# An attention and maxout kernel: its opening stage written as one list of pieces, with its PSUM places rearranged

## The chip, the cores and the metric

One NeuronCore of a Trainium2 chip runs one launch. The metric is device time in microseconds (us); less is better. Three runs of the kernel before took 813.16 to 813.38 us, with a median of 813.33.

## What is computed

```python
def mab(q, kv):                                  # scale = 1 / sqrt(128)
    s = scale * (q @ kv.transpose(0, 2, 1))
    s = s - s.max(-1, keepdims=True)
    a = np.exp(s); a /= a.sum(-1, keepdims=True) + 1e-09
    return a @ kv
h = mab(I, x)             # 32 inducing rows attend to 12544 tokens; 4 batches, 128 channels
y = mab(x, h)             # every token attends to the 32 rows of h
z = np.maximum(np.maximum(y @ w1, y @ w2), y @ w3)   # 128 -> 768
out = z @ w_out                                   # 768 -> 128
```

Everything is float32. The weights lie in memory as 64-bit floats.

## The kernel before, in words

A batch is 98 tiles of 128 tokens: group 0 has two tiles ("short": `xgs`, `xTs`), groups 1 to 6 have 16 (`xg`, `xT`). The program has two stages. The **opening stage** (`phase1_first` and the `ORDER` loop behind it) computes `h` of batch 0 from its seven groups, converts the weights from 64 to 32 bits, and makes the product `us` of `h` with the weights. The **main stage** (`main`, `advance`, `stage2`) takes 512 tokens at a time through the second attention and the maxout in 600 slots, and works out `h` of the next batch in between. Every engine runs its instructions in the order in which the code records them (`manual_schedule`), so an order is written out by hand, for the opening stage in `LOADS`, `WORK` and `ORDER`.

In the opening stage each group g goes through these steps; the letters are those of the changed list:

- l: a load of the SP queue. 0 to 6 are the token groups, 7 is w2, 8 is w_out, 9 is w1, 10 is w3. Full groups have four buffers; group 5 has one of its own, and group 6 takes that of group 1 once its sums are done.
- T: TensorE transposes 4 tiles (`transpose_x`, L343); C: ScalarE copies them out of PSUM (L345). Four of each for a full group.
- S: scores, inducing rows times tokens (`attend_products`, L353). M: their maximum on VectorE (L391). D: a column of it on ScalarE (L398). P: one small matmul that spreads it over the partitions (`attend_spread`, L405). L: the least of it on VectorE (L410).
- E: exponentials on ScalarE (L436). V: their transpose on VectorE (L465). U: the weighted sums of tokens on TensorE (`attend_sums`, L489). K: ScalarE keeps them (`attend_keep`, L502).
- w0 to w3 with a letter: conversion of a weight (0 w2, 1 w_out, 2 w1, 3 w3): t (L240), T (L244), p (L249) and r (L253) on VectorE, z (L259) on ScalarE, A (L261) an addition on GpSimd or VectorE, d (L265) on VectorE, S (L269) on GpSimd.

Then `cl`, `cw`, `cm`, c and `sg`, `ts`, `it`, `cs` combine the seven groups into `hT` (L616 to L663). Behind it come scores of batch 0 (`scores_products`, L734), four matmuls f0 to f3 to `us` (L677, `first_products`), their copies h and z (L682, L692) and differences v, scores e0, e1 of batch 1 (L353, groups 0 and 1), the copy `ek` of those (L374), the steps a and b of the second softmax of groups 0 and 1 (L747 to L783), and the first slots of the main stage (s, `advance`). The copies `pT` of finished weights (`probs`, L803) go over the SP queue.

PSUM has eight banks: `aux0`, `aux1`, `pu0`, `pu1`, `pv0`, `pv1`, `acc0`, `acc1`. Before, scores alternate between the two `aux` banks, the spread maximum has `acc0` and the sums have `acc1`.

```python
for gi in range(NG - 1):
    attend_products(0, gi + 1, bank_a[(gi + 1) % 2])
    attend_weights(0, gi)
    ...
    attend_spread(0, bank_o[0])
    attend_least(0, gi + 1)
```

Of the kernel before, what the change touches and what calls it, by code (L numbers as in the profile page):

```python
# [25 lines left out]
def kernel(ctx, tc, x, xt, ind_t, w1, w2, w3, w_out, out):  # L26
    nc = tc.nc
# [11 lines left out]
    LOADS = (0, 1, 2, 7, 3, 8, 4, 5, 9, 6, 10)  # L39

    WORK = (
        "",
        ("0t 0T 0p 0z", "0r 0A"),
        ("1t 1T 1p 1z", "1r 1A"),
        ("0d 1d", "2t"),
        ("2T 2p 2z", "2r 2A"),
        ("3t 3T 3z", "3p 2d 2S"),
        "3r",
        "3a 3d 3S",
    )  # L50
# [142 lines left out]
    raws = []  # L193
    def first_loads():
        for what in LOADS:
            if what < NG:
                xg_next[(0, what)] = load_group(0, what, pieces=4 if what == 1 else 1)
            else:
                raws.append(load_raw(srcs[what - NG]))
# [75 lines left out]
    def work(steps):  # L275
        for kind in steps.split():
            convert(int(kind[0]), kind[1])

    w2t = []

    def transpose_w2():
        for h in range(2):
            tpw = bank_v[h]
            for k in range(3):
                j = 3 * h + k
                nc.tensor.transpose(out=tpw[:, k * P : (k + 1) * P], in_=wf[:, 0, j * P : (j + 1) * P], identity=ident)
            w2h = hp.tile([P, 512], F32, name="w2h", tag="ru", bufs=3)
            nc.scalar.copy(out=w2h[:, : 3 * P], in_=tpw[:, : 3 * P])
            w2t.extend(w2h[:, k * P : (k + 1) * P] for k in range(3))
# [86 lines left out]
    def attend_max(b, gi):  # L376
# [15 lines left out]
        st["mq"] = mq  # L392

    def attend_column(b):

# [1 line left out]
        md = wk.tile([P, NQ], F32, name="md", tag="md")
        nc.scalar.mul(out=md, in_=quad, mul=st["mq"])  # L398
        st["md"] = md

    def attend_spread(b, bank=None):
# [143 lines left out]
    def phase1_first():  # L545

        start_batch(0)
        nc.sync.dma_start(out=iT, in_=ind_t)
        nc.scalar.mul(out=iT, in_=iT, mul=scale)
        first_loads()  # L550
        def half(gi, k):
            if gi < NG:
                if k == 0:
                    start_group(0, gi)
                for i in (k, k + 4):
                    transpose_x(0, gi, i)

        start_group(0, 0)
        keep_busy(6, bank_o[1])
        transpose_x(0, 0, 0)  # L560
        keep_busy(2, bank_o[1])
        attend_products(0, 0, bank_a[0])
        attend_max(0, 0)
        attend_column(0)
        half(1, 0)
        attend_spread(0, bank_o[0])
        attend_least(0, 0)
        half(1, 8)
        work(WORK[0])
        st = state[0]  # L570
        for gi in range(NG - 1):
            last = gi == NG - 2
            attend_products(0, gi + 1, bank_a[(gi + 1) % 2])
            attend_weights(0, gi)
            if gi == 2:
                keep_busy(4, bank_o[1], P)
            half(gi + 2, 0)
            attend_max(0, gi + 1)
            attend_column(0)
            half(gi + 2, 8)  # L580
            if gi > 0:
                attend_sums(0, gi - 1, bank_o[1])
                attend_keep(0, gi - 1)
            attend_transpose(0, gi)
            if not last:
                work(WORK[gi + 1][0])
            attend_spread(0, bank_o[0])
            attend_least(0, gi + 1)
            if gi == 3:
                transpose_w2()  # L590
            if last:
                prep_products()
            else:
                work(WORK[gi + 1][1])
        combine_least(st)
        work(WORK[NG - 1])
        combine_weights(st)
        attend_weights(0, NG - 1)
        keep_products()
        attend_sums(0, NG - 2, bank_o[1])  # L600
        attend_keep(0, NG - 2)
        combine_mask(st)
        combine_groups(st, range(NG - 1), bank_u[0])
        attend_transpose(0, NG - 1)
        sum_groups(st)
        attend_sums(0, NG - 1, bank_o[1])
        total_sums(st, bank_o[0])
        attend_keep(0, NG - 1)
        work(WORK[NG])
        invert_total(st)  # L610
        combine_groups(st, range(NG - 1, NG))
        combine_states(st, NQ)

# [429 lines left out]

    with tc.manual_schedule(engines=MANUAL):
        phase1_first()
        st = state[0]
        scores_products(0, 0, bank_a[0])
        scores_products(0, 1, bank_a[1])
        prep_out()
        first_products(st, 0, bank_o[0])  # L1050
        first_products(st, 1, bank_o[1])
        start_batch(1)
        load_channels(1, 0)
        load_channels(1, 1)
        load_channels(1, 2)
# [1 line left out]
        for step in ORDER.split():
            if step == "p":
                chunks[0].pT = probs(chunks[0], bank_u[0])
            elif step == "q":  # L1060
                chunks[1].pT = probs(chunks[1])
            elif step == "d":
                keep_busy(2, bank_u[(pipe["next"] + 1) % 2])
            elif step == "s":
                advance()
            elif step == "S":
                scores_products(0, 2, bank_a[0])
            elif step == "e":
                attend_products(1, 1, bank_v[1])
                attend_products(1, 0, bank_v[0])  # L1070
            elif step == "f":
                keep_scores(1)
            elif step == "g":
                attend_products(1, 2, bank_a[1])
            elif step == "m":
                more = len(st["up"])
                first_products(st, more, bank_o[more - 2])
            elif step == "c":
                first_low(st, which)
            elif step in steps:  # L1080
                next(steps[step])
            else:
                which = int(step)
                first_high(st, which)
# [59 lines left out]
```

## Time and profile before

| what | value |
|---|---|
| time of three runs | 813.16, 813.33, 813.38 us |
| span of the profiled execution, first to last instruction | 811.8 us |
| so around the span, against the median | 1.5 us |
| TensorE busy | 800.6 us, 99% of the span |
| ScalarE, GpSimd, VectorE busy | 91%, 80%, 77% |
| granted TensorE clock | 1.000 over the span |

The profile gives the span of its execution and no time of its own; the three runs stand beside it. A line of the timeline reads: start, duration, engine (PE TensorE, PEld its weight loads, ACT ScalarE, DVE VectorE, POOL GpSimd, SPq the SP queue), line, operation, output<-input, shape, count, and in brackets the idle time of that engine before it with what ended it. Busy time is a share over stages with different limits, so the opening stage (about 0 to 55 us) has to be read apart from the rest.

### The profile page before, as it was taken

The numbers are of one execution on the slowest core, as the hardware profiler recorded it, in microseconds if no ns is written. First come the engines' busy times: TensorE is split into PE (matmuls) and PEld (weight loads), VectorE is DVE, ScalarE is ACT, GpSimd is POOL, SyncE is SP. The second block draws the span as 40 slices with busy tenths as digits, with TensorE's granted clock in tenths as the row PEclk, the third lists the DMA queues.
The fourth block names the chain that finished last, engine by engine and source line by source line (L and its number), as shares of the span: only waits on it lengthen the run. The fifth ranks groups of instructions, "written<-read, shape, count | busy, mean of one in ns | idle before, by whom it ended". The sixth has DMA issues, their size and how long they took to land.

```text
span 811.8 us, 14334 instructions
## 1 busy us (share of the span) xinstructions
PE 800.6 (99%) x4561; PEld 629.4 (78%) x4561; DVE 628.0 (77%) x1067; ACT 734.8 (91%) x1532; POOL 648.2 (80%) x520
## 2 busy tenths in 40 slices
PE   8989999999999999999999999999999999999998
PEld 5758778777777787787877877878878788787887
DVE  4878878777877887877886878778778778778874
ACT  6779889899998998988998989889989999899996
POOL 1269879788788887886987978878879889788887
PEclk9999999999999999999999999999999999999999
DMA  8843234274542633533734426334223222222221
GB/s 327 318 141 111 75 122 145 85 244 157 178 134 69 192 116 103 192 117 108 233 113 123 118 99 197 112 105 134 69 77 102 66 72 78 66 87 73 62 79 52
DMA packets 52842, 102.51 MB, mean 126 GB/s; under 512 B 18208, under 2 KB 22176, under 8 KB 47520
## 3 DMA queue, kind: packets, MB, share of 16 engines
q1 hardware_dynamic: 52624, 101.47, 39.6%
q8 instruction: 36, 0.59, 0.3%
q14 instruction: 38, 0.31, 0.1%
q10 hardware_dynamic: 144, 0.13, 0.0%
HBM read 48.12 MB, written 25.69 MB: 91 GB/s over the span
## 4 chain that ended last, share of the span: by engine, by line
PE 96%; DMA 2%; SPq 1%; issue 0%; ACT 0%; DVE 0%; POOL 0%; POOLq 0%; ACTq 0%; DVEq 0%
PE acc L885 17%; PE pu L820 17%; PE pv L826 17%; PE acc L886 16%; PE acc L887 16%; PE aux L734 3%; PE acc L884 3%; PE acc L489 3%; PE aux L353 2%; DMA xg<-in_x_dram 2%; PE pu L343 0%; SPq L169 0%; PE pv L343 0%; POOL us L693 0%; PE aux L700 0%
## 5 line engine op out<-in xcount | busy, mean ns | idle before, releaser
L850 POOL TENSOR_TENSOR lows<-h,hi 128x512 fp32r<-128x512 f32 (+1 forms) x504 | 633.5, 1291 | 122.1 <-ACT hi L842 121.4
L853 DVE TENSOR_TENSOR h<-pv,ru 128x512 f32<-128x512 f32 (+1 forms) x600 | 403.4, 674 | 159.1 <-PE pv L826 99.8
L835 ACT ACTIVATE ru<-pu 128x512 f32<-128x512 f32 (+1 forms) x600 | 387.3, 645 | 51.3 <-PE pu L820 49.0
L842 ACT CAST hi<-h 128x512 fp32r<-128x512 f32 (+1 forms) x600 | 398.6, 664 | 0.3 <-DVE h L853 0.3
L820 PE MATMUL pu<-pT,us 128*128 128x512 f32 (+1 forms) x600 | 231.8, 387 | 1.8 <-ACT hi L842 0.9
L885 PE MATMUL acc<-hi,wo_hi 128*128 128x512 f32 (+1 forms) x594 | 231.8, 390 | 0.0
L826 PE MATMUL pv<-pT,us 128*128 128x512 f32 (+1 forms) x600 | 231.8, 386 | 0.1
L886 PE MATMUL acc<-hi,wo_lo 128*128 128x512 f32 (+1 forms) x594 | 228.9, 385 | 0.0
L887 PE MATMUL acc<-lows,wo_hi 128*128 128x512 f32 (+1 forms) x594 | 228.8, 385 | 0.0
L885 PEld LDWEIGHTS acc<-hi,wo_hi 128*128 128x128 f32 x594 | 111.5, 188 | 29.3 <-issue 7.5
L820 PEld LDWEIGHTS pu<-pT,us 128*128 128x128 f32 x600 | 112.5, 188 | 26.8 <-ACT ru L835 1.5
L826 PEld LDWEIGHTS pv<-pT,us 128*128 128x128 f32 x600 | 112.6, 188 | 23.7 <-DVE h L853 1.2
L887 PEld LDWEIGHTS acc<-lows,wo_hi 128*128 128x128 f32 x594 | 111.5, 188 | 22.7
L886 PEld LDWEIGHTS acc<-hi,wo_lo 128*128 128x128 f32 x594 | 111.6, 188 | 21.7
L856 DVE TENSOR_TENSOR lows<-h,hi 128x512 fp32r<-128x512 f32 x96 | 76.5, 797 | 0.8 <-ACT hi L842 0.8
L898 ACT COPY o<-acc 128x512 f32<-128x512 f32 (+1 forms) x96 | 61.6, 641 | 0.0
L884 PE MATMUL acc<-pT,us 128*128 128x512 f32 (+1 forms) x99 | 38.1, 385 | 0.0
L489 PEld LDWEIGHTS acc<-xg,aT 128*32 128x32 f32 x672 | 18.7, 110 | 9.4 <-issue 5.8
L353 PE MATMUL aux<-xT,iT 128*32 128x512 f32 x184 | 24.2, 597 | 1.7 <-ACT xT L345 1.7
L734 PE MATMUL aux<-xT,hT 128*32 128x512 f32 x192 | 25.1, 603 | 0.0
L261 POOL TENSOR_TENSOR rest<-rest,t 128x768 f32<-128x768 f32 x3 | 5.5, 1819 | 24.4 <-DVE rest L253 24.4
L489 PE MATMUL acc<-xg,aT 128*32 128x128 f32 x672 | 22.5, 273 | 0.0
(151 smaller groups left out, 446.2 us busy)
## 6 DMA issues: line engine op xcount, KB each, us to landing
out_dram<-o SPq DMA_DIRECT2D x95, 256.0 KB, 2.2
xg<-in_x_dram SPq DMA_DIRECT2D x23, 1024.0 KB, 5.9
xT<-in_xt_dram SPq DMA_DIRECT2D x18, 1024.0 KB, 5.3
pT<-ph SPq DMA_DIRECT2D x192, 64.0 KB, 2.0
pT<-pl SPq DMA_DIRECT2D x192, 64.0 KB, 2.0
raw<-in_w_dram SPq DMA_DIRECT2D x3, 768.0 KB, 8.5
us<-uh SPq DMA_DIRECT2D x24, 52.0 KB, 1.9
us<-ul SPq DMA_DIRECT2D x24, 52.0 KB, 2.6
```

The source lines that it names most:

```text
L489: nc.tensor.matmul(out=hps[q * M : (q + 1) * M, :], lhsT=aT[g][:, t * M : (t + 1) * M], rhs=xgs[g][:, t, :], start=(first[q] == k), stop=( ...
L820: nc.tensor.matmul(out=pu[:, :w], lhsT=state[c.b]["us"][:, 2 * j * P : (2 * j + 1) * P], rhs=c.pT[:, :w], start=True, stop=True)
L826: nc.tensor.matmul(out=pv[:, : d.w], lhsT=state[d.b]["us"][:, (2 * j + 1) * P : (2 * j + 2) * P], rhs=d.pT[:, : d.w], start=True, stop=True,)
L835: nc.scalar.activation(out=ru[:, :w], in_=pu[:, :w], func=AF.Relu)
L842: nc.scalar.copy(out=hi[:, : c.w], in_=h[:, : c.w])
L850: nc.gpsimd.tensor_sub(**args)
L853: nc.vector.tensor_max(out=h[:, : d.w], in0=pv[:, : d.w], in1=relus.pop(s)[:, : d.w])
L856: nc.vector.tensor_sub(**low)
L884: nc.tensor.matmul(out=to, lhsT=us[:, 2 * DF :], rhs=c.pT[:, cs], start=True, stop=False)
L885: nc.tensor.matmul(out=to, lhsT=wo_hi[:, j, :], rhs=c.hh[j][:, cs], start=False, stop=False)
L886: nc.tensor.matmul(out=to, lhsT=wo_lo[:, j, :], rhs=c.hh[j][:, cs], start=False, stop=False)
L887: nc.tensor.matmul(out=to, lhsT=wo_hi[:, j, :], rhs=c.hl[j][:, cs], start=False, stop=(j == NJ - 1))
```

## The change

`LOADS`, `WORK`, `ORDER` and `phase1_first` go, and one list `FIRST` of 245 pieces says the order of everything in the opening stage; `first` looks a piece up and records it. Copies that stood with their transposes are pieces of their own now (C, Y), and so are z and `o1`, `o2`. Scores rotate through `aux0`, `aux1` and `acc0`. The spread maxima have columns of their own (from 384) in `acc1`, and the sums have three places in `acc1` (columns 0, 128, 256), so that P, L, U and K of all groups share that one bank. Maxima of two groups can be spread together. Loads no longer follow from `start_group`: the list has them.

```diff
-    LOADS = (0, 1, 2, 7, 3, 8, 4, 5, 9, 6, 10)
...
-    ORDER = "a a a a b a a b 0 c e m b a b a f b a p b 1 c s b b b s S m b q 2 c s 3 c s g s s s"
+    FIRST = (
+        "l0 x0 li is T0.0 C0.0 l7 l1 w0t l2 l3 S0 k0 M0 w0z l10 x1 w0T k1 l4 w0p T1.4 T1.0 T1.12 l5 C1.4 C1.0 "
...
+        "P5.5 U2 M6 L5.5 w2z V4 D6 E5 K2 P6.6 L6.6 q1 U4 V5 E6 K3 U5 cl V6 U6 cw cm w2d w1z w1A c0 c1 K4 K6 "
+        "K5 c2 c3 sg ts c4 c5 w1d w3S it c6 e0 cs s0 o1 w2S s1 a a a b f0 e1 f1 b b a z0 h0 a b a a b h1 z1 b "
+        "G ek f2 q2 a b b a v0 b H pb h2 s2 o2 b s v2 v1 s f3 h3 s s n0 s pq eg s v3 s "
+    )
...
+            st["md"] = const.tile([P, NG, NQ], F32, name="md")
+            st["mq"] = {}
...
-        ahead = max(NG, b * NG + gi + 4)
-        if ahead < B * NG:
-            key = (ahead // NG, ahead % NG)
-            if key not in xg_next:
-                xg_next[key] = load_group(*key)
...
+    def attend_column(b, gi):
+
+        st = state[b]
+        nc.scalar.mul(out=st["md"][:, gi, :], in_=quad, mul=st["mq"].pop(gi))
+
+    def attend_spread(b, gi, gl, bank):
+
+        st = state[b]
+        k = slice(gi, gl + 1)
+        st["mp"] = mp = bank[:, 3 * C : 3 * C + NG * NQ].rearrange("p (g q) -> p g q", q=NQ)
+        nc.tensor.matmul(out=mp[:, k, :], lhsT=sel, rhs=st["md"][:, k, :], start=True, stop=True)
...
-    def phase1_first():
...
-            attend_spread(0, bank_o[0])
-            attend_least(0, gi + 1)
...
+            "n": lambda g: xg_next.__setitem__((1, g), load_group(1, g)),
+            "q": lambda g: load_channels(1, g),
...
+            "S": lambda g: attend_products(0, g, (*bank_a, bank_o[0])[g % 3]),
...
+            "P": lambda g, k: attend_spread(0, g, k, bank_o[1]),
+            "L": lambda g, k: attend_least(0, g, k),
...
+            "U": lambda g: attend_sums(0, g, bank_o[1], g % 3 * C),
+            "K": lambda g: attend_keep(0, g),
```

**Loads on the SP queue.** Before, from the load of group 1 (in four parts) on; `in_w_dram` is w2, then w1, then w3:

```order
L169 DMA xg<-in_x_dram 128x512 x4
L169 DMA xg<-in_x_dram 128x2048
L189 DMA raw<-in_w_dram 128x1536
L169 DMA xg<-in_x_dram 128x2048
L189 DMA raw<-in_w_out_dram 128x6x256
L169 DMA xg<-in_x_dram 128x2048
L169 DMA xg_131<-in_x_dram 128x2048
L189 DMA raw<-in_w_dram 128x1536
L169 DMA xg<-in_x_dram 128x2048
L189 DMA raw<-in_w_dram 128x1536
```

Changed; `in_w_dram` is w2, then w3, then w1, and `xg` after `in_w_out_dram` is group 6, then two groups of batch 1:

```order
L185 DMA raw<-in_w_dram 128x1536
L165 DMA xg<-in_x_dram 128x512 x4
L165 DMA xg<-in_x_dram 128x2048 x2
L185 DMA raw<-in_w_dram 128x1536
L165 DMA xg<-in_x_dram 128x2048
L165 DMA xg_170<-in_x_dram 128x2048
L185 DMA raw<-in_w_dram 128x1536
L185 DMA raw<-in_w_out_dram 128x6x256
L165 DMA xg<-in_x_dram 128x2048 x3
L176 DMA xTs<-in_xt_dram 128x256
L165 DMA xg<-in_x_dram 128x2048
L176 DMA xT<-in_xt_dram 128x2048 x2
```

w2 has moved ahead of group 1, w3 ahead of group 4, and w_out behind w1; group 6 now stands behind all four weights, where it stood ahead of w3. `xT` of group 1 of batch 1 (`q1`) stands behind three full groups of batch 1, as before.

**TensorE from the scores of group 6 on**, with the engines whose semaphores an instruction waits for. Before (`acc_85` is bank `acc0`, `acc_86` is `acc1`):

```order
L353 MATMUL aux_79<-xT,iT 32x512 [waits Activation_49]
L353 MATMUL aux_79<-xT,iT 32x512 x3
L489 MATMUL acc_86<-xg,aT 32x128 [waits DVE_49,Activation_49]
L489 MATMUL acc_86<-xg,aT 32x128 x15
L405 MATMUL acc_85<-md,sel 128x4 [waits Activation_49]
L296 MATMUL pu_82<-wf,w2h 128x128 x6
L489 MATMUL acc_86<-xg_131,aT 32x128 [waits DVE_49,Activation_49]
L489 MATMUL acc_86<-xg_131,aT 32x128 x15
L637 MATMUL pu_81<-sw,hg 128x64 [waits DVE_49,Pool_49]
```

Changed (S6, P5, U2, P6, U4, U5, U6, then c0 to c3):

```order
L349 MATMUL aux_79<-xT,iT 32x512 [waits Activation_49]
L349 MATMUL aux_79<-xT,iT 32x512 x3
L401 MATMUL acc_86<-md,sel 128x4 [waits Activation_49]
L485 MATMUL acc_86<-xg,aT 32x128 x16
L401 MATMUL acc_86<-md,sel 128x4 [waits DVE_49,Activation_49]
L485 MATMUL acc_86<-xg,aT 32x128 [waits DVE_49]
L485 MATMUL acc_86<-xg,aT 32x128 x15
L485 MATMUL acc_86<-xg_170,aT 32x128 [waits DVE_49,Activation_49]
L485 MATMUL acc_86<-xg_170,aT 32x128 x15
L485 MATMUL acc_86<-xg,aT 32x128 [waits DVE_49]
L485 MATMUL acc_86<-xg,aT 32x128 x15
L564 MATMUL pu_81<-sw,hg 128x64 [waits DVE_49,Pool_49]
```

Three sums (U4, U5, U6) stand behind the spread of the last maximum, where two stood, and the spread and the sums are in one bank.

**TensorE behind `hT`.** Before:

```order
L734 MATMUL aux_80<-xT,hT 32x512 x4
L677 MATMUL acc_85<-wcat,hT 128x512
L677 MATMUL acc_86<-wcat,hT 128x512
L353 MATMUL pv_84<-xT,iT 32x512 x4
L353 MATMUL pv_83<-xTs,iT 32x64 x4
L677 MATMUL acc_85<-wcat,hT 128x512
```

Changed:

```order
L667 MATMUL aux_80<-xT,hT 32x512 x4
L604 MATMUL acc_85<-wcat,hT 128x512
L349 MATMUL pv_84<-xT,iT 32x512 x4
L604 MATMUL acc_86<-wcat,hT 128x512
L288 MATMUL pu_82<-wf,w2h 128x128 x6
L604 MATMUL acc_85<-wcat,hT 128x512
```

The scores e1 of batch 1, which need the load `q1`, now stand ahead of f1, the short scores e0 ahead of the batch's own, and the product of w2 and w_out (L296 before) has moved behind f1. The main stage keeps its code and order.

## Rows read from the trace of the kernel before

**Rows 1.** The page: span, and busy time of each engine with its share.
```profile
span 811.8 us, 14334 instructions
PE 800.6 (99%) x4561; PEld 629.4 (78%) x4561; DVE 628.0 (77%) x1067; ACT 734.8 (91%) x1532; POOL 648.2 (80%) x520
```

**Rows 2.** Busy time of 60 to 100 us: PE, PEld, DVE, ACT, POOL; clock, DMA share, GB/s.
```profile
60.00:100.00 40.00, 40.00 (x244) 32.02 (x243) 35.47 (x57) 36.55 (x78) 37.16 (x31) 1.00 0.31 90
```

**Rows 3.** Timeline: instructions that waited for a load to land, in order.
```profile
12.56 0.56 DVE L240 TENSOR_SCALAR t<-raw 128x768 uint32<-128x768 uint32 x1 [0.80 <-DMA raw<-in_w_dram]
...
15.09 0.86 PEld L343 LDWEIGHTS pu<-ident,xg 128*128 128x128 f32 x8 [1.26 <-DMA xg<-in_x_dram]
...
17.37 0.65 DVE L240 TENSOR_SCALAR t<-raw 128x768 uint32<-128x768 uint32 x1 [0.46 <-DMA raw<-in_w_out_dram]
...
21.20 0.85 PEld L343 LDWEIGHTS pu<-ident,xg 128*128 128x128 f32 x8 [1.49 <-DMA xg<-in_x_dram]
...
25.42 0.56 DVE L240 TENSOR_SCALAR t<-raw 128x768 uint32<-128x768 uint32 x1 [0.73 <-DMA raw<-in_w_dram]
```

**Rows 4.** SP queue: issues of group 6 and of q1, and each one's time to landing.
```profile
24.24 0.33 SPq L169 DMA_DIRECT2D xg<-in_x_dram  x1
...
xg<-in_x_dram SPq DMA_DIRECT2D x1, 1024.0 KB, 4.7
...
39.06 5.41 SPq L180 DMA_DIRECT2D xT<-in_xt_dram  x2
...
xT<-in_xt_dram SPq DMA_DIRECT2D x1, 1024.0 KB, 5.9
```

**Rows 5.** Timeline from the transposes of group 6 to hT.
```profile
30.35 1.09 PE L343 MATMUL pu<-ident,xg 128*128 128x128 f32 x8
...
33.58 1.06 PE L353 MATMUL aux<-xT,iT 128*32 128x512 f32 x8
...
35.10 0.68 DVE L391 TENSOR_REDUCE mq<-aux 128x1 f32<-128x512 f32 x1
...
36.16 0.38 PE L405 MATMUL acc<-md,sel 128*128 128x4 f32 x2 [0.65 <-ACT md L398]
...
36.58 0.16 DVE L410 TENSOR_REDUCE mneg<-acc 128x1 f32<-128x4 f32 x1 [0.19 <-PE acc L405]
...
37.18 0.67 ACT L436 ACTIVATE a<-aux,mneg 128x512 f32<-128x512 f32 x1
...
37.81 0.38 DVE L626 TENSOR_TENSOR sw<-sel,w 128x224 f32<-128x224 f32 x1
37.92 1.08 PE L489 MATMUL acc<-xg,aT 128*32 128x128 f32 x32
...
38.11 0.70 DVE L465 STREAM_TRANSPOSE aT<-a 128x512 f32<-128x512 f32 x1
...
38.93 1.55 PE L637 MATMUL pu<-sw,hg 128*128 128x64 f32 x12
...
39.07 0.27 ACT L502 COPY hg<-acc 128x128 f32<-128x128 f32 x1 [0.78 <-PE acc L489]
...
41.87 0.19 DVE L657 TENSOR_SCALAR rec<-acc 128x32 f32<-128x32 f32 x1 [0.96 <-PE acc L653]
...
42.55 0.29 DVE L663 TENSOR_TENSOR hT<-pu,rec 128x128 f32<-128x128 f32 x1
```

**Rows 6.** GpSimd's addition, and VectorE's step d by source line: min/median/max ns.
```profile
20.82 1.82 POOL L261 TENSOR_TENSOR rest<-rest,t 128x768 f32<-128x768 f32 x1 [2.66 <-DVE rest L253]
...
L265 DVE SCALAR_TENSOR_TENSOR wf<-size,rest x2: 947/1294/1642, 21.8 to 23.4; 128x768 f32<-128x768 f32 x2
```

**Rows 7.** Timeline behind hT, to the first full-width matmul of the main stage.
```profile
44.01 1.98 PE L677 MATMUL acc<-wcat,hT 128*128 128x512 f32 x4
...
50.25 0.58 ACT L780 CAST ph<-aux 128x512 fp32r<-128x512 f32 x1
...
54.94 0.47 PE L820 MATMUL pu<-pT,us 128*128 128x512 f32 x1 [0.87 <-ACT hi L842]
```

More of the change, by code (lines that the diff above doesn't have):

```diff
@@ L37 @@
     MANUAL = {mybir.EngineType.PE, mybir.EngineType.Activation, mybir.EngineType.SP, mybir.EngineType.DVE, mybir.EngineType.Pool}
-    LOADS = (0, 1, 2, 7, 3, 8, 4, 5, 9, 6, 10)
[L41 to L49, printed above, removed]
+    FIRST = (
[9 rows of a table added]
     )
-    ORDER = "a a a a b a a b 0 c e m b a b a f b a p b 1 c s b b b s S m b q 2 c s 3 c s g s s s"
     STEPS2 = (3, 5, 7, 8, 9, 10, 11, 13, 14, 15)
@@ L192, with first_load @@
     srcs = [w2.bitcast(U32), w_out.bitcast(U32).rearrange("(j p) c -> p j c", p=P), w1.bitcast(U32), w3.bitcast(U32)]
[L193 to L199, printed above, removed]
+    raws = {}
+    def first_load(what):
+        if what < NG:
+            xg_next[(0, what)] = load_group(0, what, pieces=4 if what == 1 else 1)
+        else:
+            raws[what - NG] = load_raw(srcs[what - NG])
     ident = const.tile([P, P], F32, name="ident")
@@ L273, in convert, with transpose_w2, keep_w2 @@
             )
[L275 to L289, printed above, removed]
+    w2t = {}
+    def transpose_w2(h):
+        tpw = bank_v[h]
+        for k in range(3):
+            j = 3 * h + k
+            nc.tensor.transpose(out=tpw[:, k * P : (k + 1) * P], in_=wf[:, 0, j * P : (j + 1) * P], identity=ident)
+    def keep_w2(h):
+        w2h = hp.tile([P, 512], F32, name="w2h", tag="ru", bufs=3)
+        nc.scalar.copy(out=w2h[:, : 3 * P], in_=bank_v[h][:, : 3 * P])
+        w2t.update((3 * h + k, w2h[:, k * P : (k + 1) * P]) for k in range(3))
     def prep_products():
@@ L299, in keep_products, with out_high, out_low @@
         nc.scalar.copy(out=wcat[:, 2 * DF :], in_=bank_u[1][:, :C])
-    def prep_out():
+    def out_high():
+        nc.scalar.copy(out=wo_hi, in_=wf[:, 1, :].rearrange("p (j c) -> p j c", c=C))
+    def out_low():
         wo = wf[:, 1, :].rearrange("p (j c) -> p j c", c=C)
-        nc.scalar.copy(out=wo_hi, in_=wo)
         nc.gpsimd.tensor_sub(out=wo_lo, in0=wo, in1=wo_hi.bitcast(F32))
@@ L343, in transpose_x, with keep_x @@
             nc.tensor.transpose(out=tps[:, i * P : (i + 1) * P], in_=st["xg"][gi][:, k + i, :], identity=ident)
+    def keep_x(b, gi, k):
+        st = state[b]
+        n = min(4, groups[gi]["nt"] - k)
+        tps = (bank_u + bank_v)[k // 4]
         xv4 = st["xT"][gi].rearrange("p (q t l) -> p t q l", q=NQ, l=M)
@@ L391, in attend_max, with attend_least @@
         nc.vector.tensor_reduce(out=mq, in_=st["a"][gi][:, :w], axis=AX.X, op=ALU.max, negate=True)
-        st["mq"] = mq
-    def attend_column(b):
+        if b == 0:
+            st["mq"][gi] = mq
+    def attend_column(b, gi):
         st = state[b]
[L397 to L401, printed above, removed]
+        nc.scalar.mul(out=st["md"][:, gi, :], in_=quad, mul=st["mq"].pop(gi))
+    def attend_spread(b, gi, gl, bank):
         st = state[b]
-        st["mp"] = bank or spare[0]
-        nc.tensor.matmul(out=st["mp"][:, :NQ], lhsT=sel, rhs=st["md"], start=True, stop=True)
-    def attend_least(b, gi):
+        k = slice(gi, gl + 1)
+        st["mp"] = mp = bank[:, 3 * C : 3 * C + NG * NQ].rearrange("p (g q) -> p g q", q=NQ)
+        nc.tensor.matmul(out=mp[:, k, :], lhsT=sel, rhs=st["md"][:, k, :], start=True, stop=True)
+    def attend_least(b, gi, gl):
         st = state[b]
-        new, mp = st["mneg"][:, gi : gi + 1], st["mp"]
-        nc.vector.tensor_reduce(out=new, in_=mp[:, :NQ], axis=AX.X, op=ALU.min)
+        k = slice(gi, gl + 1)
+        nc.vector.tensor_reduce(out=st["mneg"][:, k], in_=st["mp"][:, k, :], axis=AX.X, op=ALU.min)
     def exchange_maxima(b, gi):
@@ L543, in keep_busy @@
             nc.tensor.matmul(out=bank[:, at_:], lhsT=ident_r, rhs=rhs, start=True, stop=True)
-    def phase1_first():
[L547 to L565, printed above, removed]
-        attend_spread(0, bank_o[0])
[L567 to L587, printed above, removed]
-            attend_least(0, gi + 1)
[L589 to L612, printed above, removed]
     def combine_least(st):
@@ L690, in first_low, with first_copy @@
         n = up.shape[1]
-        uf = hp.tile([P, 512], F32, name="uf", tag="uf", bufs=2)
+        uf = st["uf"][which]
+        nc.gpsimd.tensor_sub(out=us[low], in0=uf[low, :n], in1=us.bitcast(F32)[low])
+    def first_copy(st, which):
+        up, _ = st["up"][which]
+        low = slice(2 * M, P)
+        n = up.shape[1]
+        uf = st.setdefault("uf", {})[which] = hp.tile([P, 512], F32, name="uf", tag="uf", bufs=2)
         nc.scalar.copy(out=uf[low, :n], in_=up[low])
-        nc.gpsimd.tensor_sub(out=us[low], in0=uf[low, :n], in1=us.bitcast(F32)[low])
     def combine_products(st, bank):
@@ L1042, in main @@
                     over = c
-    with tc.manual_schedule(engines=MANUAL):
[L1045 to L1055, printed above, removed]
-        steps = {"a": scores_steps(0, 0), "b": scores_steps(0, 1)}
[L1057 to L1084, printed above, removed]
@@ new lines, in first @@
+    def first(step, st):
+        kind, rest = step[0], step[1:]
+        n = [int(k) for k in rest.split(".")] if rest.replace(".", "").isdigit() else []
+        two = {
+            "li": lambda: nc.sync.dma_start(out=iT, in_=ind_t),
+            "is": lambda: nc.scalar.mul(out=iT, in_=iT, mul=scale),
+            "cl": lambda: combine_least(st),
+            "cw": lambda: combine_weights(st),
+            "cm": lambda: combine_mask(st),
+            "sg": lambda: sum_groups(st),
+            "ts": lambda: total_sums(st, bank_o[1][:, 3 * C + NG * NQ :]),
+            "it": lambda: invert_total(st),
+            "cs": lambda: combine_states(st, NQ),
+            "o1": out_high,
+            "o2": out_low,
+            "next": lambda: start_batch(1),
+            "e0": lambda: attend_products(1, 0, bank_v[0]),
+            "e1": lambda: attend_products(1, 1, bank_v[1]),
+            "eg": lambda: attend_products(1, 2, bank_a[1]),
+            "ek": lambda: keep_scores(1),
+            "s": advance,
+            "a": lambda: next(steps["a"]),
+            "b": lambda: next(steps["b"]),
+            "k0": lambda: keep_busy(6, bank_o[1]),
+            "k1": lambda: keep_busy(2, bank_o[1]),
+            "k2": lambda: keep_busy(4, bank_o[1], P),
+            "G": prep_products,
+            "H": keep_products,
+        }
+        one = {
+            "l": first_load,
+            "n": lambda g: xg_next.__setitem__((1, g), load_group(1, g)),
+            "q": lambda g: load_channels(1, g),
+            "x": lambda g: start_group(0, g),
+            "T": lambda g, k: transpose_x(0, g, k),
+            "C": lambda g, k: keep_x(0, g, k),
+            "S": lambda g: attend_products(0, g, (*bank_a, bank_o[0])[g % 3]),
+            "M": lambda g: attend_max(0, g),
+            "D": lambda g: attend_column(0, g),
+            "P": lambda g, k: attend_spread(0, g, k, bank_o[1]),
+            "L": lambda g, k: attend_least(0, g, k),
+            "E": lambda g: attend_weights(0, g),
+            "V": lambda g: attend_transpose(0, g),
+            "U": lambda g: attend_sums(0, g, bank_o[1], g % 3 * C),
+            "K": lambda g: attend_keep(0, g),
+            "y": transpose_w2,
+            "Y": keep_w2,
+            "c": lambda g: combine_groups(st, [g], bank_u[0]),
+            "s": lambda g: scores_products(0, g, bank_a[g % 2]),
+            "f": lambda k: first_products(st, k, bank_o[k % 2]),
+            "h": lambda k: first_high(st, k),
+            "z": lambda k: first_copy(st, k),
+            "v": lambda k: first_low(st, k),
+        }
+        if step == "pb":
+            chunks[0].pT = probs(chunks[0], bank_u[0])
+        elif step == "pq":
+            chunks[1].pT = probs(chunks[1])
+        elif kind == "w":
+            convert(int(rest[0]), rest[1])
+        elif step in two:
+            two[step]()
+        else:
+            one[kind](*n)
@@ L1085 @@
+    with tc.manual_schedule(engines=MANUAL):
+        start_batch(0)
+        steps = {"a": scores_steps(0, 0), "b": scores_steps(0, 1)}
+        for step in FIRST.split():
+            first(step, state[0])
         assert next(steps["a"], None) is next(steps["b"], None) is None
```

5 rows, old and new, of the table FIRST are left out of this document.

## The prediction

> **What bounds the kernel now.** I read the page first. TensorE is busy for 99% of the span [rows 1], and from 60 to 100 us for 40.00 of 40.00 us at full clock [rows 2]. Behind the opening stage there is no slack on TensorE, and the change leaves the main stage as it is. So whatever the opening stage gains or loses in the start of the full-width slots, the total gains or loses one for one. That start is the first 512-column `pu` matmul, at 54.94 us [rows 7]. Next I read the opening stage as a timeline. Up to 25.4 us, five instructions stand still until a load lands [rows 3]: the loads set the pace there. Behind that, the chain runs from group 6 to `hT`: transposes at 30.35, scores at 33.58, maximum at 35.10, its spread at 36.16, exponentials at 37.18, then sums and combination, and `hT` at 42.55 [rows 5]. Group 6 had landed 4.7 us after its issue at 24.24, at 28.9 [rows 4], so its last 1.4 us were no wait for data. Third comes what lies between `hT` and 54.94 [rows 7]. I follow the changed order along these three parts. The sum is made against the span of 811.8 us; the median stands 1.5 us above it, and I add the difference to the median.
>
> **The loads.** By their sizes, the changed queue carries the same bytes up to the end of w1 as the old one, since w3 has the place of w_out. So w1 lands where it did, at about 25.3 [rows 3]. What is new is w_out behind it. It took 2.3 us behind a token group, 15.09 to 17.37 [rows 3]. The lower end is three quarters of the 2.5 us that one megabyte took (12.56 to 15.09), which is 1.9; the upper end is the 3.8 us between 17.37 and 21.20. I take 2.3, the row of the same tensor: w_out at 27.6. Group 6 follows with 2.5, at 30.1 (29.7 to 31.4). Its buffer is free by then: it needs U1 some 4.7 us earlier, and U1 now stands ahead of the transposes of group 5. Loading weights first therefore delays group 6 by 1.2 us against 28.9. The transposes are only as late as before (30.35), since TensorE no longer has a backlog: from T6 to S6 it took 3.2 us [rows 5], so S6 could run at 33.3.
>
> **VectorE behind w_out.** Its queue now has the first step of w_out (w1t) ahead of eight others. From the landing it runs w1t, w2p (of the same size, so the same price), a least, a maximum, w1T, w2r, V3, a maximum and a least: 0.56 twice, 0.16 twice, 0.68 twice, 0.95 twice and 0.70 [rows 3, 5, 6], 5.4 in all. Each begins about 0.08 before the last has ended (37.81 plus 0.38 against 38.11 [rows 5]), so 4.8: VectorE is done at 32.5. U3 waits for that least and stands ahead of S6 on TensorE. U3 runs to 33.6 (32 rows in 1.0, from 37.92 to 38.93 [rows 5]), and S6 starts at 33.6, as before. M6 needs no wait for a conversion as it had: 34.7 to 35.4. From the start of the maximum to its spread it was 1.06 us [rows 5], so P6 could run at 35.75, ahead of the old 36.16 by 0.4.
>
> **One bank for maxima and sums.** Before, P6 in `acc0` began as soon as its column was there [rows 5]. Now P, L, U and K are all in `acc1`, and the waits in the built program (shown with the change) go from reader to writer of the whole bank: P6 waits for VectorE and ScalarE, U5 for ScalarE as well. By their counts, L5 waits for the end of U2, P6 for the copy K2, and U4 for L6. So: P5 0.3 and U2 1.0 behind S6's 1.0 end at 36.0; L5 0.16, E5 0.67 and K2 0.27 [rows 5] stand one behind the other, and P6 runs at 37.15. That costs 1.4 against 35.75 (between nothing, if K2 were already done, and that). L6 is done at 37.75, U4 behind it at 38.9. K3 takes 0.27, then U5 and U6 with 1.05 each: 41.4. Four of the products c take 1.0 of the 1.5 for six [rows 5], the total 0.3, three more 0.75: 43.4, and `hT` could come at 43.5. From P6 to `hT` that is the 6.4 us it was. Three sums stand there instead of two, but no product waits any more for a late copy. What the three places were to hide, U4 and U5 ahead of the last maximum, they don't hide.
>
> [...]
>
> **Step d of w_out beside GpSimd.** w1d now stands behind w2d, whose result GpSimd takes up at once for 1.8 us. By the counts above V6 follows U4 (38.9), then `sw` 0.38 and w2d 0.95: GpSimd runs from 40.9 to 42.7, and w1d starts at 41.1 beneath it. The same operation took 0.95 alone but 1.64 when it began at 21.82 beneath a GpSimd addition that ended at 22.64 [rows 6]: 0.82 beneath and 0.82 behind it, so hardly anything was done beneath. By that row w1d ends at 43.5, not 42.05. `rec` stands behind it, and from `rec` to `hT` it was 0.68 [rows 5]: `hT` at 44.2. Bounds: 43.5 (no hindrance) and 44.2; I take 44.2, the row of the same operation on the same tile. That is 1.65 later than 42.55.
>
> [...]
>
> **Behind `hT`.** f1 ended 3.45 us behind the start of `hT` (44.01 plus 1.98 [rows 7]). Now e1 stands between f0 and f1 and adds 1.0: 48.65. e1 needs q1, issued when U5 is done (40.3) and landing 5.9 later [rows 4], at 46.2, just before e1's turn at 46.65; if a load ahead of it takes 3.8, it is 0.9 late. Behind f1 ScalarE has five copies, then `ph`: some 2.2 by the 0.58 of a wide one [rows 7], so 50.95. VectorE's chain from `hT` to `ph` was 7.7 [rows 5, 7], so 51.9 less the 0.3 of a step that moved behind it: that one decides. From `ph` to the full width it was 4.7 (50.25 to 54.94 [rows 7]): 56.3. But the first chunk's narrow slots, which began before `ph`, now all begin behind it (0 to 0.6, the width of one wide copy); I put 0.5. So 56.8 against 54.94, **1.85 us later: 815.2**. All else in the list (single pieces for copies, spreads of two groups, `keep_busy` moved) lies before 25 us, under the loads, and costs nothing; if it did, it would show as transposes of group 4 well behind their landing.
>
> **Rivals.** (1) *It evens out.* GpSimd doesn't hold w1d (0.7 less), w_out takes 1.9 (0.4 less), `ph` decides alone (0.5 less): 0.25 later, 813.6. For it: 1.64 is one instance. Against: all three would have to go together; two of them still leave about 1. (2) *The loads lose more.* If one load up to w_out takes 3.8 as between 17.37 and 21.20 [rows 3], the chain behind w_out moves by 1.5, and q1 may add to it: 816.7. (3) *Faster.* The waits go by place, not by bank. Then P6 is at 35.75, U4 and U5 fill TensorE under L6 and E6, U6 ends at 39.1, `hT` comes 2.1 later at 41.2, and with U3 clear of the least of group 4 0.3 earlier: 40.9, 1.65 before the old one, so 811.7. It decides wherever P6 starts before K2. The built program's waits speak against it.
>
> **How the numbers follow.** A measurement of this kernel can tell 0.2%, 1.63 us, from no change: the bounds are 811.7 and 814.96. My forecast has 0.56, and of it 0.43 is above the bound; rival 2 has 0.17, rival 1 0.20, rival 3 0.07. So slower 0.60, same 0.33, faster 0.07. The range goes from rival 1's side, 813.4, to just beyond rival 2, 817.0.
>
> **What would show it.** In the profile after: w_out's first step behind a wait for its load near 27.6; P6 near 37 behind ScalarE's `hg`, not its column; U4 behind VectorE's least; w1d longer than 1.5 us beneath GpSimd; `hT` near 44; full-width `pu` near 56.8. I am wrong if P6 follows its column and `hT` comes before 42.5, or if the main stage's TensorE shows gaps that it didn't have.

## The result, and the profile after

The changed kernel takes **817.37 us** (median of 4 runs, 816.82 to 818.42) where the old one takes 813.28 beside it: a ratio of **1.0052, interval 1.0039 to 1.0066**. It is slower, by about 4.1 us, where 1.85 was forecast; 817.37 lies just above the range's end of 817.0. The profiled run of 816.85 us has a span of 815.1, 3.3 above the old one's [rows 1].

The page of the changed kernel, its span and the busy time of its engines:

```profile
span 815.1 us, 14329 instructions
PE 800.4 (98%) x4561; PEld 630.3 (77%) x4561; DVE 631.1 (77%) x1067; ACT 734.6 (90%) x1532; POOL 646.9 (79%) x520
```

TensorE does the same work, 800.4 us against 800.6 [rows 1]; it only starts the main stage later. The next view is busy time by stretch of the changed kernel; the columns are PE, PEld, DVE, ACT, POOL, then the granted clock, the DMA share and GB/s.

```profile
35.00:40.00 5.00, 3.11 (x70) 2.72 (x70) 3.47 (x9) 3.00 (x8) 2.58 (x2) 0.84 1.01 410
40.00:45.00 5.00, 4.87 (x80) 3.84 (x72) 3.76 (x8) 1.44 (x4) 1.81 (x1) 0.81 1.00 363
45.00:50.00 5.00, 4.18 (x27) 1.62 (x20) 4.59 (x11) 2.44 (x5) 2.02 (x2) 1.00 0.80 283
50.00:55.00 5.00, 3.53 (x24) 1.79 (x23) 4.18 (x7) 3.22 (x10) 2.36 (x2) 1.00 0.07 19
...
60.00:100.00 40.00, 40.00 (x250) 32.23 (x249) 35.69 (x57) 36.58 (x78) 36.82 (x31) 1.00 0.30 85
```

From 60 to 100 us TensorE is busy throughout at a granted clock of 1.00, as before [rows 2]. From 35 to 40 TensorE is busy for only 3.11 of 5 us, and part of the time from 35 to 45 has a lower granted clock (0.84 and 0.81 in the two stretches, 0.50 from 38.5 to 41.5; the old trace has 1.00 in both). So the loss lies between group 6 and the main stage. This is the timeline of that part of the changed kernel, up to `hT`; beside [rows 3] and [rows 5] it shows what each step waits for.

```profile
27.01 0.56 DVE L235 TENSOR_SCALAR t<-raw 128x768 uint32<-128x768 uint32 x1 [0.64 <-DMA raw<-in_w_out_dram]
...
32.66 1.04 PE L349 MATMUL aux<-xT,iT 128*32 128x512 f32 x8
...
33.63 0.39 PE L401 MATMUL acc<-md,sel 128*128 128x4 f32 x2
...
36.28 0.39 PE L401 MATMUL acc<-md,sel 128*128 128x4 f32 x2 [1.25 <-ACT hg L498]
...
36.92 1.08 PE L485 MATMUL acc<-xg,aT 128*32 128x128 f32 x32 [0.25 <-DVE mneg L406]
...
38.38 3.62 PE L485 MATMUL acc<-xg,aT 128*32 128x128 f32 x64 [0.39 <-ACT hg L498]
...
40.07 1.81 POOL L264 TENSOR_TENSOR wcat<-dst,wf 128x768 f32<-128x768 f32 x1 [2.49 <-DVE lw L574]
40.18 2.52 DVE L260 SCALAR_TENSOR_TENSOR wf<-size,rest 128x768 f32<-128x768 f32 x1
...
43.27 0.19 DVE L584 TENSOR_SCALAR rec<-acc 128x32 f32<-128x32 f32 x1 [0.57 <-PE acc L580]
...
43.97 0.29 DVE L590 TENSOR_TENSOR hT<-pu,rec 128x128 f32<-128x128 f32 x1
```

S6 is there at 32.66, 0.9 earlier than before [rows 5]: no loss by the new order of the loads is to be seen. Then the loss begins. TensorE stands still for 1.25 us ahead of P6 (36.28) until a ScalarE copy of sums is done, and for 0.25 ahead of U4 (36.92) until a least is; U5 and U6 together take 3.62 where one took 1.08; w_out's step d takes 2.52 beneath the GpSimd subtraction that began 0.11 before it. Step d is done at 42.70, and VectorE then waits 0.57 for TensorE's total (`rec`, 43.27), which stands behind U6: here the sums ended last, not step d. `hT` comes 1.42 later than in [rows 5]. Behind it, in the same timeline:

```profile
47.36 1.06 PE L349 MATMUL pv<-xT,iT 128*32 128x512 f32 x8 [0.81 <-DMA xT<-in_xt_dram]
...
48.36 1.12 PE L604 MATMUL acc<-wcat,hT 128*128 128x512 f32 x2
...
49.28 1.82 POOL L298 TENSOR_TENSOR wo_lo<-wf,wo_hi 128x768 fp32r<-128x768 f32 x1
...
49.37 1.76 DVE L693 TENSOR_SCALAR rs<-rs 128x16 f32<-128x16 f32 x1
...
52.95 0.59 ACT L713 CAST ph<-aux 128x512 fp32r<-128x512 f32 x1 [1.36 <-DVE aux L710]
...
58.10 0.39 PE L753 MATMUL pu<-pT,us 128*128 128x512 f32 x1
```

From `hT` to `ph` it is 8.98 us, where [rows 5, 7] have 7.70. An addition of 16 columns to `rs`, 0.16 us long in the old trace, takes 1.76: it ends at 51.13, as soon as GpSimd's `wo_lo` ends at 51.10. The full-width slots begin at 58.10, 3.16 later than in [rows 7], and the span grows by about as much.

### The profile page after: what moved, and what is told of

It is laid out like the page before. It is cut to its first block, busy times and chain, and to the rows that moved or that the text cites. A ratio compares the mean times of both kernels' runs of the same rounds, so it can differ in the third digit from the quotient of the medians.

```text
span 815.1 us, 14329 instructions
## 1 busy us (share of the span) xinstructions
PE 800.4 (98%) x4561; PEld 630.3 (77%) x4561; DVE 631.1 (77%) x1067; ACT 734.6 (90%) x1532; POOL 646.9 (79%) x520
## 4 chain that ended last, share of the span: by engine, by line
PE 94%; DMA 3%; DVE 2%; SPq 0%; ACT 0%; issue 0%; ACTq 0%; DVEq 0%
PE acc L818 17%; PE pu L753 17%; PE pv L759 16%; PE acc L819 16%; PE acc L820 16%; PE aux L667 3%; PE acc L485 3%; PE acc L817 3%; DMA raw<-in_w_out_dram 2%; PE aux L349 2%; DMA xg<-in_x_dram 1%; PE aux L633 0%; DVE rs L693 0%; PE pu L564 0%; PE aux L820 0%; PE aux L819 0%
## 5 line engine op out<-in xcount | busy, mean ns | idle before, releaser
L349 PE MATMUL aux<-xT,iT 128*32 128x512 f32 x168 | 22.0, 595 | 0.0
```

## The experiments

After the result, my theory (A below) was that three things cost the time: waits by bank up to `hT`, two VectorE steps held beneath GpSimd, and e1's wait for its transfer. The rivals were that one of them alone decides, that TensorE's clock does, or that a further bound lies behind them. Each kernel below is the changed one with pieces of its list moved, unless it says otherwise; each is timed beside the old kernel on the same chip (812.84, 813.2 and 812.77 in the three groups), and all ratios are to that. "P6 to `hT`" and the like are read from each profile, since the whole opening moves by about a microsecond from one profile to the next.

**1. wo_lo early.**

```diff
-c6 e0 cs s0 o1 w2S s1
+c6 e0 cs s0 o1 o2 w2S s1
...
-h2 s2 o2 b s v2
+h2 s2 b s v2
```

> One step moved: GpSimd makes wo_lo right behind wo_hi (before its first uf piece), as the old program did, and not in the middle of the second softmax chain. Theory A (GpSimd's 1.82 us addition holds VectorE's 128x16 addition to rs, which took 1.76 instead of 0.17): that addition falls to about 0.2, the copy ph begins near 51.4 instead of 52.95, the full-width slots near 56.6 instead of 58.10, and the time is 1.5 us less, 815.8. Rival B (the late transfer of the second group decides: f1 waits behind e1 for it): ph doesn't move by more than 0.5, and the time by no more than 0.5.

Measured: 816.91, ratio 1.0049 (1.0037 to 1.0061), no gain that can be told. `rs` took 0.18, as expected of theory A, and yet `hT` to `ph` was 8.44. The move was badly placed: on GpSimd's queue `wo_lo` now stood ahead of the last subtraction into `wcat`, and f0 waited 1.31 us for that. The subtraction came later, so step d had no GpSimd operation beside it and took 0.95; P6 to `hT` was 7.64 all the same, against 7.69 in the change.

**2. The step d of w_out first.**

```diff
-cm w2d w1z w1A c0 c1
+cm w1z w1A w1d w2d c0 c1
...
-c5 w1d w3S
+c5 w3S
```

> One step moved: VectorE's last step of w_out stands ahead of the last step of w1, so that it can't run beneath the GpSimd subtraction that the latter releases. Theory A (behind P6 two things end nearly together: the held step at 42.70, and group 6's sums, which the halved clock stretches to 42.0): the step takes 0.95 instead of 2.52, but hT moves by no more than 0.2, and the time by less than 0.3. Rival B (as predicted blind, the held step decides alone): hT 0.6 to 0.7 earlier, near 43.3, and the time 0.6 less.

Measured: 818.45, ratio 1.0061 (1.0049 to 1.0073). P6 to `hT` went from 7.69 to 6.55, more than either theory said, since here the clock stayed at 1.00 up to 45 as well. The time gained nothing: e1 stood 2.22 us for its transfer, f1 behind it, and the clock fell later (0.85 and 0.80 from 45 to 55). An earlier `hT` alone was of no use here. The addition to `rs` fell beneath `wo_lo` again, but later in it:

```profile
47.51 1.81 POOL L298 TENSOR_TENSOR wo_lo<-wf,wo_hi 128x768 fp32r<-128x768 f32 x1
...
48.75 0.60 DVE L693 TENSOR_SCALAR rs<-rs 128x16 f32<-128x16 f32 x1
```

It began 1.24 behind the start of `wo_lo` and took 0.60, until 0.03 behind its end.

**3. Sums in banks of their own.**

```diff
-"U": lambda g: attend_sums(0, g, bank_o[1], g % 3 * C),
+"U": lambda g: attend_sums(0, g, {2: bank_v[0], 4: bank_v[1], 5: bank_u[1], 6: bank_v[0]}.get(g, bank_o[1]), g % 3 * C),
```

> One thing changed: the sums of groups 2, 4, 5 and 6 go to three banks that stand empty by then (the transposes' banks) instead of the bank in which the maxima are spread. Theory A (readers and writers wait for each other by the bank): P6 follows its column, near 35.0 instead of 36.28, U4 follows its weights, near 36.0 instead of 36.92, U6 ends near 39.5 instead of 42.0, hT comes near 42.3 instead of 43.97 (the held step of w_out then decides), and the time is 1.3 to 1.7 less. Rival B (the bank costs nothing, the late maximum and the clock do): P6 and hT stay within 0.3, and so does the time.

Measured: 815.82, ratio 1.0034 (1.0023 to 1.0046). The timeline of this kernel, P5 and P6, then step d, `hT`, and e1:

```profile
32.72 0.39 PE L401 MATMUL acc<-md,sel 128*128 128x4 f32 x2
...
34.05 0.39 PE L401 MATMUL acc<-md,sel 128*128 128x4 f32 x2
...
37.99 2.51 DVE L260 SCALAR_TENSOR_TENSOR wf<-size,rest 128x768 f32<-128x768 f32 x1
...
41.09 0.29 DVE L590 TENSOR_TENSOR hT<-pu,rec 128x128 f32<-128x128 f32 x1
...
46.04 1.53 PE L349 MATMUL pv<-xT,iT 128*32 128x512 f32 x8 [2.37 <-DMA xT<-in_xt_dram]
```

P6 comes 1.33 us behind P5 instead of 2.65: the bank costs about 1.3 there, and rival B falls. `hT` comes at 41.09, ahead of the old one; but e1 then stands 2.37 for its transfer, the clock is at 0.66 from 45 to 50, `rs` takes 0.80 beneath `wo_lo`, and `hT` to `ph` grows to 10.47. Much of the gain is eaten there; the interval of the time overlaps that of the change.

**4. Matmuls to fill TensorE ahead of P6.**

```diff
-E5 K2 P6.6
+E5 K2 k3 P6.6
...
+"k3": lambda: keep_busy(4, bank_u[1]),
```

> Four 512-column matmuls into an empty bank are added ahead of P6, where TensorE stood still from 35.0 to 36.3; their result is not used. Theory A (the granted clock fell to its lower level behind that idle time, and stretched U5 and U6 from 2.2 to 3.6): the granted clock stays at 1.00 in 35 to 45, U5 and U6 take about 2.2, and hT is earlier by 0.5, near 43.5, where the held step of w_out then decides; the time 0.5 less. Rival B (the clock is the whole loss up to hT): hT 1.4 earlier and the time with it. Rival C (the clock falls for another reason): it still falls, and the time stays or grows by up to 0.3.

Measured: 816.62, ratio 1.0046 (1.0033 to 1.0059): not to be told from the change's 1.0052. The stretches of this kernel, and its U5 and U6:

```profile
35.00:40.00 5.00, 4.24 (x105) 3.32 (x103) 3.53 (x10) 2.91 (x11) 2.52 (x3) 1.00 1.02 418
40.00:45.00 5.00, 3.88 (x39) 1.99 (x37) 3.37 (x7) 1.25 (x4) 1.09 (x1) 0.76 0.91 338
```

```profile
37.59 1.95 PE L485 MATMUL acc<-xg,aT 128*32 128x128 f32 x64 [0.39 <-ACT hg L498]
```

U5 and U6 are at 1.95 and P6 to `hT` at 7.01 (7.69 in the change), so the slower clock was worth 0.7 there; but it was at 0.76 in the next stretch. That the added matmuls kept it up is not shown: in experiments 2 and 7 TensorE stands still for the same 1.25 us ahead of P6, and the clock stays at 1.00 up to 45 without them. What the clock costs in all stays open. `rs` was not held here (it began 0.23 ahead of `wo_lo` and took 0.17), and yet `hT` to `ph` was 8.56: the scores of batch 0 took 1.93 and f0 1.66, where the change has 1.04 and 1.12.

**5 to 7. wo_lo behind the last subtraction; e1 behind f1; both.**

```diff
-c6 e0 cs s0 o1 w2S s1
+c6 e0 cs s0 o1 w2S o2 s1
...
-h2 s2 o2 b s v2
+h2 s2 b s v2
```

```diff
-f0 e1 f1 b
+f0 f1 b
...
-G ek f2
+G e1 ek f2
```

> The step wo_lo on GpSimd stands right behind the last weight subtraction into wcat, so that neither waits in the other's way (in the run before this one it stood ahead of that subtraction and made f0 wait for it). Theory A (the hold of VectorE's addition to rs costs 1.5 of the way from hT to ph): rs 128x16 takes 0.2, hT to ph goes from 8.98 to about 7.7, the time is 1.0 to 1.4 less than the change's. Theory C (e1, which waits until the second group's transfer lands near 47, holds f1 and with it ScalarE's queue ahead of ph): hT to ph stays at 8.4 or more and the time gains at most 0.5.

> One step moved: e1, the matmul that waits for the second group's transfer, stands behind f1 and the weight product instead of ahead of f1. Theory C (that wait holds f1, ScalarE's copies behind it, and so ph): f1 starts at once behind f0, near 46.5 instead of 48.36, ph comes about 1.0 earlier, the time is 1.0 less. Theory A (the softmax chain decides, held by GpSimd): f1 is earlier too, but ph stays near 52.9 for a hT near 43.97, and the time within 0.3.

> Both of the last two moves together. If either one alone was hidden by the other (two bounds that end together), hT to ph comes to about 7.7 here, as in the old program, and the time is 1.3 to 1.7 less than the change's, more than the two alone add up to. If they are independent, the sum of the two. If neither matters, no change.

Measured: wo_lo alone 815.6, ratio 1.0030 (1.0018 to 1.0042); e1 alone 816.61, 1.0039 (1.0026 to 1.0052); both 815.15, 1.0026 (1.0016 to 1.0035). Only the interval of both together lies clear of the change's. From `hT` to `ph` they have 8.03, 8.98 and 7.41 us; the first lies between the 7.7 of theory A and the 8.4 of theory C. With e1 alone moved, the hold is still there:

```profile
47.98 1.81 POOL L298 TENSOR_TENSOR wo_lo<-wf,wo_hi 128x768 fp32r<-128x768 f32 x1
48.06 1.75 DVE L693 TENSOR_SCALAR rs<-rs 128x16 f32<-128x16 f32 x1
...
51.64 0.59 ACT L713 CAST ph<-aux 128x512 fp32r<-128x512 f32 x1 [2.27 <-DVE aux L710]
```

With both moved it is gone:

```profile
42.55 0.29 DVE L590 TENSOR_TENSOR hT<-pu,rec 128x128 f32<-128x128 f32 x1
...
42.96 1.82 POOL L298 TENSOR_TENSOR wo_lo<-wf,wo_hi 128x768 fp32r<-128x768 f32 x1 [1.81 <-ACT wo_hi L294]
...
47.96 0.17 DVE L693 TENSOR_SCALAR rs<-rs 128x16 f32<-128x16 f32 x1
...
49.96 0.59 ACT L713 CAST ph<-aux 128x512 fp32r<-128x512 f32 x1 [0.70 <-DVE aux L710]
```

The hold beneath GpSimd ends last, worth 0.95; once it is gone, f1 behind e1's wait ends last, worth 0.62 more; e1 alone moves `ph` by nothing. In the traces that is what two bounds one behind the other do. In the times the intervals are too wide to tell it from a plain sum.

**8. Four moves together:** 2, 3, 5 and 6.

> Four moves together: sums in banks of their own, the last step of w_out ahead of that of w1, wo_lo behind the last subtraction into wcat, e1 behind f1. If the bank waits, the two holds beneath GpSimd and the wait for the transfer are the whole loss: hT near 40.8, ph near 48.7, the full-width slots near 53.7 against 54.94 in the old program, and the time near 811.5 to 812.5 where the old one has 813.0: slightly faster. If a further bound lies behind them (the loads of the next batch in the queue, the slower clock, or the transfers of ph and pl), hT moves as said but the full-width slots stay near 56 to 57 and the time above 814.5.

Measured: 812.86, ratio 1.0001 (0.9991 to 1.0011): the old program's time. Its timeline, step d, `hT` and the first full-width matmul:

```profile
37.22 0.95 DVE L260 SCALAR_TENSOR_TENSOR wf<-size,rest 128x768 f32<-128x768 f32 x1
...
40.50 0.29 DVE L590 TENSOR_TENSOR hT<-pu,rec 128x128 f32<-128x128 f32 x1
...
55.08 0.39 PE L753 MATMUL pu<-pT,us 128*128 128x512 f32 x1
```

P6 to `hT` is 6.12. The four together take back the whole loss, but not more, although `hT` is 2 us ahead of [rows 5]: e0 stood 1.16 for its transfer ahead of the scores, and f0 and f1 took 3.45 for both (1.98 in [rows 7]).

**9. Three of the four:** without the move of step d.

> The four moves of the run before without the one of w_out's last step: it runs again beneath the GpSimd subtraction. If that hold costs what it did in the change's trace (the step 2.52 instead of 0.95, with sums in their own banks now alone ahead of hT), hT comes 0.6 to 1.0 later than with all four, and the time is 813.5 to 814 against 812.9. If something else decides behind hT (the transfer for e1, the narrow slots), no difference over 0.3.

Measured: 813.75, ratio 1.0008 (0.9996 to 1.0019). P6 to `hT` is 7.06 instead of 6.12, with step d at 2.51 again: the hold costs 0.94 there, where nothing else ends last. What it costs in time is not shown: the ratio moves by 0.0007, some 0.6 us, with intervals that overlap, and the full-width slots of this profile begin at 54.95, no later than in experiment 8.

**10. The old program with wo_lo late.** The subtraction moves into a function of its own, called behind the first uf piece.

```diff
-ORDER = "a a a a b a a b 0 c e m
+ORDER = "a a a a b a a b 0 c w e m
```

> The old program with one step moved: the GpSimd subtraction for wo_lo stands behind the first uf piece, as in the change, so that it begins near 47.8, where VectorE makes its addition to rs (47.95, 0.16). Theory A (the hold is a cost of its own): the addition takes about 1.7, hT to ph goes from 7.7 to about 9.2, ph to near 51.8, and the time is 1.0 to 1.5 more than the old program's. Rival (the hold shows only together with the other delays): the full-width slots move by less than 0.3 and the time stays.

Measured: 814.98, ratio 1.0020 (1.0007 to 1.0034): the old program made slower, by 1.6 us by the ratio (0.6 to 2.8). Its timeline:

```profile
41.43 0.29 DVE L666 TENSOR_TENSOR hT<-pu,rec 128x128 f32<-128x128 f32 x1
...
46.72 1.82 POOL L307 TENSOR_TENSOR wo_lo<-wf,wo_hi 128x768 fp32r<-128x768 f32 x1
...
46.83 1.74 DVE L763 TENSOR_SCALAR rs<-rs 128x16 f32<-128x16 f32 x1
...
50.39 0.59 ACT L783 CAST ph<-aux 128x512 fp32r<-128x512 f32 x1 [1.16 <-DVE aux L780]
```

`hT` to `ph` is 8.96 where it was 7.70 [rows 5, 7]; the rest of the chain is as it was (P6 to `hT` 6.39, as in [rows 5]). One move puts the hold into the old program and makes this stretch 1.26 longer, as in the change (8.98 for 7.70).

**11 and 12. e0 behind f1 as well; and the short group's probabilities early again.**

```diff
-c6 e0 cs s0
+c6 cs s0
...
-f0 f1 b
+f0 f1 e0 b
```

```diff
-z0 h0 a b a a b h1 z1 b G e1 ek f2 q2 a b b a v0 b H pb h2 s2 b s v2 v1 s f3 h3 s s n0 s
+z0 h0 a b a a b a h1 z1 a b G H pb v0 v1 e1 f2 q2 b b ek b s b h2 s v2 s2 s f3 h3 s n0 s
```

> The four moves, and e0 (which with an early hT waits for its transfer until 41.6, ahead of the scores) behind f1. If the order of TensorE behind hT still decides: s0 and s1 1.0 earlier, ph near 48.6, the time up to 0.8 less than with four, 812.2. If the narrow slots behind ph or the transfers decide: the time within 0.3 of 812.9.

> As the run with e0 behind f1, and the short group's probabilities and the first narrow slots stand ahead of ph again, as in the old program (pb near 47 instead of 50.1). If the narrow slots, all behind ph, decide when the full-width slots begin (55.08 with four), they begin near 53.3, and the time is 811.3 to 812.0, less than either program's. If the transfers of ph and pl decide, near 53.9 and 811.8 to 812.4. If neither, no less than 812.7.

Measured: 812.35, ratio 0.9992 (0.9982 to 1.0003), for e0 behind f1; 814.05, ratio 1.0011 (1.0001 to 1.0021), with the early probabilities. The first has `ph` at 48.02 and the full-width slots at 53.49, 1.45 before [rows 7]; it is the fastest of all, clearly ahead of the change, and not to be told from the old program. The second fell to the last case of its expectation. Its narrow slots were done by 53, as meant, but the full-width slots waited until 54.54 for the last piece of `pl`, which landed 3.6 us after its issue where 2.0 is usual (below), and a late piece of `pl` cost TensorE 0.76 once more at 81.

## Why the prediction was wrong

The sign was right. The step that failed is the way from `hT` to `ph`; ahead of it another step ended last than was forecast, which an early P6 hid.

- **The loads.** w_out's first step at 27.01 (27.6 forecast), S6 at 32.66 (33.6): a little early, no loss. Rival 2 gave a time near the measured one, but its reason is wrong.
- **One bank.** The waits are where they were forecast: P6 behind the copy K2, U4 behind L6. The price of 1.4 against its column measured about 1.3: TensorE stood still for 1.25 ahead of P6, and P6 behind P5 went from 2.65 to 1.33 (experiment 3). Rival 3 needed P6 ahead of K2, and falls.
- **P6 to `hT`.** Forecast 7.05, measured 7.69; 7.01 in experiment 7, where the granted clock was 1.00 from 35 to 45, and in experiment 4, where it was 1.00 from 35 to 40. The term for U5 and U6 was 2.1 and measured 3.6: the granted clock was 0.50 from 38.5 to 41.5 in this profile, and I hadn't priced that. Why the clock fell stays open. In this profile it fell behind the stop of 1.25 ahead of P6; behind the same stop it stayed at 1.00 up to 45 in experiments 2 and 7. The profile of experiment 7:

```profile
35.54 0.39 PE L401 MATMUL acc<-md,sel 128*128 128x4 f32 x2 [1.25 <-ACT hg L498]
...
37.65 1.96 PE L485 MATMUL acc<-xg,aT 128*32 128x128 f32 x64 [0.39 <-ACT hg L498]
```

  With P6 0.87 earlier than forecast, `hT` came at 43.97 for 44.2: two errors cancelled, which is luck. P6 moves with the profile; in the five others with the same order up to there it came at 35.01 to 35.85.
- **Step d beneath GpSimd.** 2.52, of which 0.82 lay behind GpSimd's end, as in [rows 6]. It was priced at 0.7 as the step that ends last, and is worth 0.94 up to `hT` when it does (experiments 8 and 9). In the change it did not: `rec` waited 0.57 more for the total behind the slow sums, and with step d at 0.95 the way from P6 to `hT` was the same (7.64, experiment 1).
- **Behind `hT`: the step that failed.** I took VectorE's 7.7 of the old trace from `hT` to `ph`, less 0.3: 7.4. It measured 8.98. In the timeline of the old kernel the two operations stood 3.4 us apart:

```profile
42.76 1.81 POOL L304 TENSOR_TENSOR wo_lo<-wf,wo_hi 128x768 fp32r<-128x768 f32 x1
...
47.95 0.16 DVE L760 TENSOR_SCALAR rs<-rs 128x16 f32<-128x16 f32 x1
```

  The change moves `wo_lo` from right behind `hT` to the place where VectorE adds to `rs`. I looked for operations beneath GpSimd at w_out's step d and not here, and I carried a chain over as a whole though one engine beside it had a new order. Without that hold and with e1 behind f1 the stretch is 7.41 (experiment 7), the forecast's number. That its time is 815.15, for 815.2 forecast, is chance: its P6 is 1.6 early, and its full-width slots begin 6.54 behind `ph`, for 5.2 forecast. Experiment 10 shows the hold by itself. Its length follows from where the addition falls: 1.74 to 1.76 at the start of `wo_lo`, 0.80 and 0.60 in the middle of it (experiments 3 and 2), 0.17 ahead of it (experiment 4). In the five held cases it ended 0.02 to 0.03 behind the end of `wo_lo`, where step d of the change ended 0.82 behind GpSimd's end.
- **e1.** I put its wait at up to 0.9 and then let VectorE decide over it. It measured 0.81. That VectorE decides was right for the change (experiment 6 alone moves `ph` by nothing), but only because of the hold: with `wo_lo` moved, the queue behind e1 ended last, by 0.62 (experiments 5 and 7).
- **From `ph` on.** Forecast 5.2, measured 5.15. The main stage is unchanged.

In legs: 0.87 early at P6, 0.64 late to `hT`, 1.58 late to `ph`, 0.05 early behind it: 1.30, and 56.8 plus 1.30 is 58.10. Another 0.5 is that the profiled run lies below the median of its four, and some 0.4 lies behind that start and around the span.

## What to carry to other kernels

When a change moves an operation on GpSimd, look at every VectorE operation that falls beneath its new place, the smallest too: one of 0.16 us took 1.76. A chain's length may be taken over from the old trace only if the queues beside it keep their order. And an instruction that waits for a load, put ahead in an in-order queue, swallows what is gained upstream: four moves together took back the 0.5% of this change, but an earlier `hT` alone was worth nothing (experiment 2, where e1 stood 2.22 us for its transfer).

## What was not expected of the hardware

In the six us from `ph` on, a 64 KB transfer of `ph` or `pl` landed 1.9 to 2.0 us after its issue, but some three in a row took 2.5 to 3.8. In the traces of both kernels and of experiments 1, 2, 4 to 7, 9, 11 and 12, the late ones stand around the one packet of 0.02 MB of the queue of kind "instruction" (q8) that comes there, and there are no others. The view of DMA in experiment 12, from the issue of the late `pl` to the full-width slots, and that transfer with the one before it:

```profile
q8 instruction: 1, 0.02, 2.3%
```

```profile
L736 SPq DMA_DIRECT2D pT<-pl x2: 541/561/581, 50.2 to 50.8; - x2
...
DMA to landing us min/median/max: 1.9/2.7/3.6
```

Where the packet meets the last `pl` of the first full-width slot (experiments 1, 4, 6, 7 and 12), that slot begins 5.8 to 6.5 us behind `ph`; in the change, and in 5, 9 and 11, it is 5.15 to 5.5 (experiment 2 has 6.1 without it, with the clock at 0.80 from 50 to 55). So where that packet falls went with a difference of up to about a microsecond, which may be part of why single moves didn't add up. That the packet causes the delay was not tried apart: the traces show the two together.
